# The three-bit rounding of the weights' lower words on VectorE, and the first tiles' steps listed anew, in an attention and SoLU feed-forward kernel

## The chip, the core and the metric

The kernel runs on one NeuronCore of a Trainium2 chip. A core has TensorE (PE in the profile: matmuls, with PEld for their weight loads), VectorE (DVE), ScalarE (ACT), GpSimd (POOL) and SyncE (SP, which here only issues DMAs). Each engine works through its own instructions in order; engines wait for one another by semaphores. The metric is the time of one execution in microseconds (us) on the device, as the median of several runs. Lower is better.

## The reference

Attention within chunks of 64 tokens, over 8 batches, 8 heads, 576 tokens and head size 64; its output, as 4608 rows of 512, goes through a feed-forward layer with a SoLU and a normalisation between two matrix products:

```python
scores = scale * np.matmul(q_c, k_c.transpose(0, 1, 2, 4, 3))
attn = softmax(scores)                      # over the 64 keys of the chunk
x = (attn @ v_c) as [4608, 512]
h = x @ w_in                                # 512 -> 1024
solu = h * softmax(h)
ln = (solu - mu) / np.sqrt(var + 1e-06) * g_ln
return (ln @ w_out).astype(np.float32)      # 1024 -> 512
```

The weights `w_in` and `w_out` come as 64-bit floats, q, k and v as 32-bit floats.

## The kernel before

**Tiles.** The 4608 rows are 36 tiles of 128 rows, numbered 0 to 35. Each tile goes through the same chain: q and k turned (head size on the partitions), 32 small score matmuls, softmax, the attention turned, 32 small value matmuls, `ffn_in` (L459: 24 matmuls of 128x512, since each operand is split into a high and a low part and three of the four products are taken), the SoLU (`solu_a` L479: a maximum over the row on VectorE, the exponential on ScalarE; `solu_b` L491: a product on VectorE, then a scale and shift called "Y ident" below), the result turned and split (`z_transpose` L562 or `z_turn` L527 with `z_split` L554), and `ffn_out` (24 matmuls, in three thirds of 8), scaled and stored.

**Weights.** The 64-bit weights are made into float pairs on the chip, in eight units of 1 MiB: units 0 to 3 are `w_in`, 4 to 7 `w_out`. A unit is loaded (`load_pair` L149, word P in the list below), its upper words are clamped and scaled (`unit_scale` L174, word c: min and max, then a ScalarE step called "prelu" below), its lower words are rounded to three bits (`unit_bits` L185, word b), both are joined on VectorE (`unit_join` L193, C), copied as the high part on ScalarE (`unit_high` L206, t), and the low part is the difference on VectorE (`unit_low` L219, d). The scaled unit lies in the tile `w_a`, of which there are two buffers, so a unit's c waits for the d of the unit two before it; the rounded words lie in `w_b`.

**Two parts of the program.** Tiles 5 to 35 have their `ffn_in` in a loop with a fixed order. All before it, which is the work on the weights, the attention of the first tiles, the `ffn_in` of tiles 0 to 4 and the `ffn_out` of tiles 0 and 1, is listed by hand in the string `START` (L18). Each word names a step and a tile or unit; a step of several parts stands once for each part, and every instruction is kept in that order on its engine. So `START` is an order for each of the five engines. The letters: n loads q and k of a tile in their natural layout, N turns one of them on TensorE and then evicts it (N:5:0 is q of tile 5), S scores, A softmax up to the exponential, B its sum and division, T turns the attention, V values with the split of x into high and low, M `ffn_in`, X `solu_a`, Y `solu_b`, R variance, z turns half of a result on TensorE, F one third of `ffn_out`, o store, Z, U and K turns by VectorE for the loop, v loads v, Q and q load q and k of a whole batch, w issues that many matmuls whose result nobody reads. F counts through: the first three are tile 0, the next three tile 1.

**Which engine.** `MOVED` (L34) names the words that do not run on their usual engine: c and b run on VectorE unless listed as `pool`, an eviction (N, z) on ScalarE unless listed as `dve`, Y ident on ScalarE unless listed. Before, b:0, b:1 and b:3 run on VectorE and the other five b on GpSimd; all eight c run on GpSimd.

**What ties the steps.** `ffn_in` writes the only buffer `ph` (L461), which is free again when Y of the tile before has read it on VectorE. The turned tiles of N, T and z share two PSUM banks (`bank`, L120) in rotation. The natural loads have two buffers, so n of a tile waits for the N of the tile two before it, and every load behind it on SP's queue waits too. `ffn_out` reads one pair `z_h`, `z_l`.

Of the kernel before, what the change touches and what calls it, by code (L numbers as in the profile page):

```python
# [15 lines left out]


START = """  # L18
n:0 P:0 P:0 n:1 P:1 w:5 N:0:0 N:0:0 w:1 N:0:1 N:0:1 w:3 S:0 n:2 c:0 A:0 A:0 w:7 N:1:0 b:0 v:0
c:1 c:0 B:0 w:2 N:1:1 N:1:0 N:1:1 C:0 P:2 w:3 S:1 t:0 c:2 T:0 T:0 c:1 A:1 A:1 w:4 N:2:0 w:2  # L20
N:2:1 n:3 N:2:0 b:1 w:2 V:0 P:3 N:2:1 S:2 d:0 C:1 t:1 V:0 b:2 v:1 B:1 n:4 w:2 T:1 T:1 d:1 A:2
c:2 A:2 V:0 C:2 w:9 N:3:1 N:3:1 N:3:0 N:3:0 M:0 M:0 B:2 b:3 t:2 S:3 n:5 c:3 c:3 d:2 C:3 V:1
N:4:0 N:4:0 t:3 T:2 N:4:1 N:4:1 n:6 A:3 A:3 d:3 M:0 B:3 N:5:1 T:2 M:0 N:5:0 P:4 V:1 S:4 N:6:0
N:5:1 N:5:0 X:0 X:0 v:2 g N:6:1 N:6:1 A:4 A:4 S:5 Y:0 c:4 c:4 T:3 T:3 V:1 A:5 A:5 N:6:0 b:4 n:7
C:4 P:5 Y:0 t:4 M:1 R:0 B:4 b:5 V:2 V:2 T:4 N:7:1 v:3 X:1 X:1 P:7 N:7:1 V:2 S:6 c:5 Y:1 c:5 T:4
d:4 v:6 v:7 B:5 V:3 Y:1 C:5 z:0:0 z:0:0 M:2 V:3 N:7:0 t:5 P:6 c:7 c:7 z:0:0 z:0:1 d:5 v:5 X:2
N:7:0 v:4 z:0:1 F X:2 V:3 z:0:1 c:6 c:6 Y:2 b:6 z:1:1 T:5 b:7 Q:2 q:8 T:5 C:7 Y:2 V:4 C:6 M:3
t:6 A:6 t:7 d:6 q:8 d:7 z:1:0 n:8 R:1 q:8 V:4 V:4 F F X:3 X:3 V:5 z:1:0 z:1:0 S:7 Y:3 Y:3 A:7
q:8 Z:2 A:7 Z:3 A:6 M:4 B:7 z:1:1 z:1:1 F F B:6 R:2 X:4 X:4 K:9 N:8:0 F Y:4 Y:4 U:6 U:7 V:5 o:0
o:1 V:5 N:8:0 R:4 N:8:1 N:8:1 R:3  # L30
"""


MOVED = """  # L34
N:6:0=dve N:8:1=dve Y:0=dve Y:4=pool b:2=pool b:4=pool b:5=pool b:6=pool b:7=pool c:0=pool
c:1=pool c:2=pool c:3=pool c:4=pool c:5=pool c:6=pool c:7=pool z:1:0=dve
"""


# [784 lines left out]
```

## Time and profile before

| | us |
|---|---|
| median of 3 runs | 488.02 (487.26 to 488.04) |
| the profiled execution | 488.82 |
| its span, first to last instruction | 487.0 |
| TensorE busy in the span | 468.7 |
| VectorE busy | 372.5 |
| ScalarE busy | 257.5 |
| GpSimd busy | 159.0 |

The span is the part of an execution that the profiler sees; 1.8 us lie around it. "Busy" is the time in which at least one instruction of the engine is under way. In the timeline a row is one instruction, or several like ones in a row, with its start and its length, and in brackets how long the engine sat idle before it and what released it. In the chain of waits each row is a piece of the chain that ended last, followed back from the end of the program.

### The profile page before, as it was taken

The page shows a single profiled execution, that of the slowest core. Times are in us where ns is not written, and L with a number is a line of the kernel's source. Part 1 is how long each engine was busy: PE and PEld are TensorE (multiplying, and loading weights), DVE is VectorE, ACT ScalarE, POOL GpSimd, SP SyncE. Part 2 cuts the span into 40 slices and gives each one's busy share as a digit, 9 for nine tenths or more (in the row PEclk, how much of TensorE's full clock was granted, in tenths as well). Part 3 has the DMA queues.
Part 4 walks back from the last instruction along what each step waited for, and adds up shares of the span by engine and source line. Part 5 has one row for each costly group of instructions (what it writes and reads, how often), then busy time and mean ns, then how long its engine had stood idle before and what let it go on. Part 6 is the DMA issues. An engine that isn't in the chain of part 4 may idle for free.

```text
span 487.0 us, 11097 instructions
## 1 busy us (share of the span) xinstructions
PE 468.7 (96%) x4208; PEld 384.7 (79%) x4208; DVE 372.5 (76%) x518; ACT 257.5 (53%) x424; POOL 159.0 (33%) x300
## 2 busy tenths in 40 slices
PE   8888887999999999999999999999999999999997
PEld 6666666888888888888888888888888888888876
DVE  3878759888869988888787879797979797954541
ACT  3867657564545564646464646464646464645452
POOL 1324570724231523232333323232323232323330
PEclk9989998999999999999999999999999999999999
DMA  9999994568776788687618596858762626153222
GB/s 261 276 201 263 238 153 62 157 106 193 141 191 125 191 153 194 121 181 151 186 35 209 96 203 129 206 97 178 154 173 48 170 56 164 47 150 84 74 60 86
DMA packets 194468, 72.57 MB, mean 149 GB/s; under 512 B 178224, under 2 KB 178992, under 8 KB 194032
## 3 DMA queue, kind: packets, MB, share of 16 engines
q1 hardware_dynamic: 187312, 58.23, 54.1%
q0 software_dynamic: 6528, 12.86, 10.4%
q8 instruction: 33, 0.54, 0.5%
q10 hardware_dynamic: 576, 0.79, 0.4%
q14 instruction: 19, 0.16, 0.1%
HBM read 36.70 MB, written 9.44 MB: 95 GB/s over the span
## 4 chain that ended last, share of the span: by engine, by line
PE 84%; POOL 4%; ACT 4%; DMA 3%; DVE 2%; issue 2%; SPq 1%; ACTq 0%; POOLq 0%; DVEq 0%
PE po L54 38%; PE ph L54 37%; PE tp L54 4%; PE sx L54 4%; POOL w_b L54 3%; DMA nat<-in_q_dram 2%; DMA w_raw<-in_moe_w_out_dram 1%; SPq L54 1%; ACT wo_h L54 1%; POOL w_a L54 1%; DVE w_a L54 1%; ACT z L54 0%; DVE h_nmax L54 0%; ACT sq L54 0%; ACT w_a L54 0%
## 5 line engine op out<-in xcount | busy, mean ns | idle before, releaser
L54 PE MATMUL po<-wo_l,z_h 128*128 128x512 f32 (+1 forms) x288 | 114.0, 396 | 2.4 <-DVE wo_l L54 2.4
L54 PE MATMUL ph<-wi_l,x_h 128*128 128x512 f32 x288 | 113.4, 394 | 1.5 <-DVE z L54 1.3
L54 ACT ACTIVATE z<-ph,h_nmax 128x1024 f32<-128x1024 f32 x36 | 40.2, 1116 | 137.6 <-DVE h_nmax L54 135.7
L54 PE MATMUL ph<-wi_h,x_h 128*128 128x512 f32 x288 | 112.6, 391 | 0.0
L54 PE MATMUL po<-wo_h,z_l 128*128 128x512 f32 (+1 forms) x288 | 112.3, 390 | 0.0
L54 PE MATMUL po<-wo_h,z_h 128*128 128x512 f32 (+1 forms) x288 | 112.1, 389 | 0.0
L54 POOL DMA_DIRECT2D z_t<-z_b x144 | 71.6, 505 | 32.1 <-DVE z_b L54 26.9
L54 POOL TENSOR_TENSOR u<-ssq,eps 128x1 f32<-128x1 f32 x36 | 6.8, 190 | 219.3 <-ACT sq L54 219.2
L54 PE MATMUL ph<-wi_h,x_l 128*128 128x512 f32 x288 | 78.3, 390 | 0.0
L54 DVE TENSOR_REDUCE h_nmax<-ph 128x1 f32<-128x1024 f32 x36 | 44.0, 1222 | 32.8 <-PE ph L54 32.8
L54 PEld LDWEIGHTS po<-wo_l,z_h 128*128 128x128 f32 x288 | 54.3, 189 | 14.8 <-DVE wo_l L54 2.8
L54 PEld LDWEIGHTS ph<-wi_l,x_h 128*128 128x128 f32 x288 | 54.3, 189 | 13.2 <-issue 1.4
L54 PEld LDWEIGHTS po<-wo_h,z_l 128*128 128x128 f32 x288 | 54.5, 189 | 11.8 <-DVE z_l L54 0.4
L54 PEld LDWEIGHTS ph<-wi_h,x_l 128*128 128x128 f32 x288 | 54.3, 189 | 11.4
L54 PEld LDWEIGHTS ph<-wi_h,x_h 128*128 128x128 f32 x288 | 54.4, 189 | 11.1
L54 PEld LDWEIGHTS po<-wo_h,z_h 128*128 128x128 f32 x288 | 54.4, 189 | 10.5
L54 DVE TENSOR_TENSOR z_l<-z_t,z_h 128x1024 fp32r<-128x1024 f32 (+1 forms) x37 | 42.1, 1137 | 25.4 <-ACT z_h L54 24.1
L54 DVE SCALAR_TENSOR_TENSOR z<-ph,z 128x1024 f32<-128x1024 f32 x36 | 43.9, 1221 | 13.6 <-ACT z L54 13.4
L54 ACT ACTIVATE z<-z,z_sum 128x1024 f32<-128x1024 f32 x34 | 39.2, 1153 | 23.5 <-DVE z L54 22.9
L54 DVE STREAM_TRANSPOSE z_b<-z 128x1024 f32<-128x1024 f32 x34 | 41.1, 1210 | 3.2 <-ACT z L54 3.1
L54 ACT CAST z_h<-z_t 128x1024 fp32r<-128x1024 f32 (+1 forms) x37 | 35.9, 971 | 6.5 <-PE po L54 6.5
L54 ACT ACTIVATE o_sb<-po,r 128x512 f32<-128x512 f32 (+1 forms) x36 | 24.3, 675 | 27.4 <-POOL r L54 18.6
(77 smaller groups left out, 609.5 us busy)
## 6 DMA issues: line engine op xcount, KB each, us to landing
out_dram<-o_sb SPq DMA_DIRECT2D x33, 256.0 KB, 2.5
v_sb<-in_v_dram SPq DMA_DIRECT2D x32, 256.0 KB, 4.5
z_t<-z_b SPq DMA_DIRECT2D x128, 64.0 KB, 2.9
z_t<-z_b POOLq DMA_DIRECT2D x128, 64.0 KB, 2.7
q_st<-in_q_dram SPq DMA_DIRECT2D x96, 72.0 KB, 3.0
k_st<-in_k_dram SPq DMA_DIRECT2D x96, 72.0 KB, 3.1
w_raw<-in_moe_w_out_dram SPq DMA_DIRECT2D x4, 1024.0 KB, 8.2
attn_t<-a_b SPq DMA_DIRECT2D x60, 64.0 KB, 4.0
```

The lines of the kernel that those rows point to most:

```text
L54: ins = make(*args, **kwargs)
```

## The change

Only the two strings differ. In `MOVED`, b:2, b:4, b:6 and b:7 are no longer listed, so that they run on VectorE; b:5 stays on GpSimd. Y ident of tile 0 goes from VectorE to GpSimd, that of tile 3 from ScalarE to VectorE and that of tile 4 from GpSimd to VectorE. The evictions N:6:0, N:8:1 and z:1:0 go from VectorE to ScalarE, N:0:1 and N:8:0 from ScalarE to VectorE.

`START` has the same steps in another order. It begins with unit 1 instead of unit 0, and its load stands ahead of the first loads of q and k. Unit 5 is loaded ahead of unit 4 and unit 6 ahead of unit 7; the number of idle matmuls (w) is 40 in both. The first lines and those around units 4 to 7:

```diff
 START = """
-n:0 P:0 P:0 n:1 P:1 w:5 N:0:0 N:0:0 w:1 N:0:1 N:0:1 w:3 S:0 n:2 c:0 A:0 A:0 w:7 N:1:0 b:0 v:0
+P:1 b:1 n:0 w:11 N:0:0 N:0:0 n:1 w:2 N:0:1 N:0:1 c:1 c:1 C:1 t:1 P:0 P:0 c:0 w:3 S:0 N:1:0
...
-N:5:1 N:5:0 X:0 X:0 v:2 g N:6:1 N:6:1 A:4 A:4 S:5 Y:0 c:4 c:4 T:3 T:3 V:1 A:5 A:5 N:6:0 b:4 n:7
-C:4 P:5 Y:0 t:4 M:1 R:0 B:4 b:5 V:2 V:2 T:4 N:7:1 v:3 X:1 X:1 P:7 N:7:1 V:2 S:6 c:5 Y:1 c:5 T:4
-d:4 v:6 v:7 B:5 V:3 Y:1 C:5 z:0:0 z:0:0 M:2 V:3 N:7:0 t:5 P:6 c:7 c:7 z:0:0 z:0:1 d:5 v:5 X:2
-N:7:0 v:4 z:0:1 F X:2 V:3 z:0:1 c:6 c:6 Y:2 b:6 z:1:1 T:5 b:7 Q:2 q:8 T:5 C:7 Y:2 V:4 C:6 M:3
-t:6 A:6 t:7 d:6 q:8 d:7 z:1:0 n:8 R:1 q:8 V:4 V:4 F F X:3 X:3 V:5 z:1:0 z:1:0 S:7 Y:3 Y:3 A:7
-q:8 Z:2 A:7 Z:3 A:6 M:4 B:7 z:1:1 z:1:1 F F B:6 R:2 X:4 X:4 K:9 N:8:0 F Y:4 Y:4 U:6 U:7 V:5 o:0
-o:1 V:5 N:8:0 R:4 N:8:1 N:8:1 R:3
+Y:0 S:4 N:6:0 N:6:0 N:5:1 V:2 A:4 V:2 V:2 T:3 T:3 M:1 A:4 g B:4 c:5 N:5:1 c:4 c:4 z:0:1 z:0:1
+b:4 N:6:1 N:6:1 n:7 v:3 v:4 S:5 X:1 X:1 T:4 T:4 N:7:1 N:7:1 b:5 z:0:1 A:5 A:5 V:3 P:6 c:6 Y:1
+Y:1 V:3 P:7 C:4 C:5 z:0:0 z:0:0 M:2 t:4 B:5 R:0 d:4 t:5 V:3 Q:2 q:8 z:0:0 c:7 N:7:0 N:7:0 S:6
+v:7 q:8 V:4 X:2 d:5 X:2 Y:2 T:5 T:5 V:4 b:6 b:7 c:6 v:5 C:6 c:7 C:7 t:6 q:8 z:1:1 n:8 F z:1:0
+t:7 R:1 d:6 d:7 M:3 X:3 X:3 F F v:6 Y:2 z:1:0 V:4 A:6 A:6 Y:3 Y:3 S:7 z:1:0 V:5 M:4 A:7 z:1:1
+o:0 R:2 B:6 A:7 z:1:1 Z:2 q:8 Z:3 F X:4 X:4 B:7 F F N:8:1 Y:4 V:5 V:5 U:6 U:7 N:8:1 R:3 Y:4
+N:8:0 R:4 N:8:0 K:9 o:1
 """
...
 MOVED = """
-N:6:0=dve N:8:1=dve Y:0=dve Y:4=pool b:2=pool b:4=pool b:5=pool b:6=pool b:7=pool c:0=pool
-c:1=pool c:2=pool c:3=pool c:4=pool c:5=pool c:6=pool c:7=pool z:1:0=dve
+N:0:1=dve N:8:0=dve Y:0=pool Y:3=dve Y:4=dve b:5=pool c:0=pool c:1=pool c:2=pool c:3=pool
+c:4=pool c:5=pool c:6=pool c:7=pool
 """
```

What the list gives each engine around this place, read off word by word:

- GpSimd before: c0 c1 c2 b2 c3 c4 b4, the variance R0, b5 c5 c7 c6 b6 b7, R1 R2. After: c1 c0 c2 c3 c5, Y ident of tile 0, c4 b5 c6 R0 c7 R1 R2.
- VectorE after, from X:1 to X:3: X1, low half of z0:1, A5, Y1, C4 C5 B5 d4, low part of x3, low half of z0:0, X2 d5 Y2 b6 b7 C6 C7 d6 d7 X3.
- TensorE after, from M:1: M1, z0:1, N6:1, S5, T4, N7:1, V3, z0:0, M2, N7:0, S6, V4, T5, z1:1, F, z1:0, M3, F F, S7, V5, M4, F F F, N8:1, N8:0, then the loop with tile 5. Before: M1, V2, T4, N7:1, S6, V3, z0:0, M2, N7:0, z0:1, F, z1:1, T5, V4, M3, z1:0, F F, V5, S7, M4, F F, N8:0, F, N8:1.
- SP before: n0 P0 n1 P1 n2 v0 P2 n3 P3 v1 n4 n5 n6 P4 v2 g n7 P5 v3 P7 v6 v7 P6 v5 v4, then batch 2 with n8. After: P1 n0 n1 P0 P2 v0 n2 n3 P3 n4 v1 n5 n6 v2 P5 P4 g n7 v3 v4 P6 P7, then batch 2 with v7, v5, n8 and v6 among it.

More of the change, by code (lines that the diff above doesn't have):

```diff
@@ L18 @@
 START = """
-n:0 P:0 P:0 n:1 P:1 w:5 N:0:0 N:0:0 w:1 N:0:1 N:0:1 w:3 S:0 n:2 c:0 A:0 A:0 w:7 N:1:0 b:0 v:0
[L20 to L23, printed above, removed]
-N:5:1 N:5:0 X:0 X:0 v:2 g N:6:1 N:6:1 A:4 A:4 S:5 Y:0 c:4 c:4 T:3 T:3 V:1 A:5 A:5 N:6:0 b:4 n:7
@@ new lines @@
+N:1:0 A:0 A:0 N:1:1 d:1 N:1:1 P:2 w:8 S:1 B:0 v:0 n:2 c:0 b:0 c:2 w:3 T:0 T:0 A:1 A:1 C:0 w:6
+V:0 c:2 t:0 B:1 w:6 N:2:1 V:0 N:2:1 b:2 V:0 N:2:0 N:2:0 n:3 w:1 N:3:0 N:3:0 S:2 C:2 d:0 P:3 T:1
+N:3:1 t:2 M:0 M:0 n:4 A:2 v:1 N:3:1 n:5 c:3 c:3 N:4:0 S:3 T:1 b:3 d:2 M:0 C:3 A:3 t:3 A:2 N:4:1
+N:4:1 d:3 N:4:0 V:1 V:1 N:5:0 n:6 v:2 N:5:0 A:3 M:0 B:2 T:2 V:1 P:5 T:2 X:0 X:0 B:3 P:4 c:5 Y:0
+Y:0 S:4 N:6:0 N:6:0 N:5:1 V:2 A:4 V:2 V:2 T:3 T:3 M:1 A:4 g B:4 c:5 N:5:1 c:4 c:4 z:0:1 z:0:1
+b:4 N:6:1 N:6:1 n:7 v:3 v:4 S:5 X:1 X:1 T:4 T:4 N:7:1 N:7:1 b:5 z:0:1 A:5 A:5 V:3 P:6 c:6 Y:1
```

## The prediction

> **What bounds the kernel now.** I read the page, then the chain of waits, then busy time by stage.
>
> ```profile
> span 487.0 us, 11097 instructions
> PE 84%; POOL 4%; ACT 4%; DMA 3%; DVE 2%; issue 2%; SPq 1%; ACTq 0%; POOLq 0%; DVEq 0%
> ```
>
> TensorE carries 84% of the chain. The rest has to be looked for where TensorE waits. I cut the span where the `ffn_in` of tiles 0, 1, 2, 3, 4, 5 begin (M0 to M5). Columns: stretch and length, then busy time (count) of PE, PEld, DVE, ACT, POOL, granted clock, DMA share, GB/s.
>
> ```profile
> 0.00:23.51 23.51, 20.07 (x209) 15.07 (x209) 13.71 (x20) 14.55 (x24) 5.82 (x14) 1.00 1.00 262
> 23.51:40.43 16.92, 13.91 (x187) 11.15 (x186) 13.27 (x19) 11.12 (x19) 4.92 (x3) 0.90 0.95 214
> 40.43:51.85 11.42, 9.20 (x134) 7.28 (x132) 8.91 (x15) 7.88 (x15) 7.24 (x5) 1.00 1.05 292
> 51.85:65.02 13.17, 10.55 (x80) 8.13 (x80) 10.21 (x14) 10.30 (x18) 7.62 (x5) 1.00 1.00 192
> 65.02:81.49 16.47, 12.82 (x109) 9.80 (x109) 10.75 (x15) 7.84 (x15) 5.74 (x4) 0.90 0.81 124
> 81.49:93.31 11.82, 11.82 (x56) 9.79 (x57) 11.53 (x18) 6.27 (x12) 5.70 (x11) 1.00 0.37 98
> 93.31:461.00 367.69, 367.67 (x3324) 304.60 (x3323) 296.48 (x411) 189.69 (x307) 116.83 (x253) 1.00 0.63 141
> ```
>
> From 93.31 TensorE is never idle for 367.7 us, and the change leaves that loop alone. So the change is worth what it shifts M5, less what the loop then has to wait for. In the first 93.31 us, TensorE idles in every stage but the sixth, most between M3 and M4. Chain and TensorE timeline say why:
>
> ```profile
> 40.96 3.72 POOL w_b L54
> 49.53 2.37 POOL w_b L54
> 62.58 3.71 POOL w_b L54
> 66.36 3.73 POOL w_b L54
> 74.51 0.49 PE L54 MATMUL po<-wo_l,z_h 128*128 128x512 f32 x1 [2.35 <-DVE wo_l L54]
> ```
>
> GpSimd's rounding is on the chain four times, 13.5 us in all. The last two keep the low parts of units 6 and 7 from `ffn_out`: TensorE idles 2.35 us at 74.51, and the stage's mean clock of 0.90 is that of 3.3 us at half clock (2 x 0.10 x 16.47), which cost half of that.
>
> **The change, part by part.** Prices first.
>
> ```profile
> L54 POOL TENSOR_SCALAR w_b<-w_raw x5: 3700/3717/3730, 21.9 to 66.4; 128x1024 uint32<-128x1024 uint32 x5
> L54 DVE TENSOR_SCALAR w_b<-w_raw x3: 682/682/687, 9.6 to 28.4; 128x1024 uint32<-128x1024 uint32 x3
> L54 POOL TENSOR_SCALAR z<-z,z_sum 128x1024 f32<-128x1024 f32 x1 | 1.1, 1138 | 2.3 <-DVE z L54 2.3
> L54 DVE TENSOR_SCALAR z<-z,z_sum 128x1024 f32<-128x1024 f32 x1 | 0.7, 748 | 0.0
> L54 DVE SCALAR_TENSOR_TENSOR w_a<-w_a,w_b 128x1024 uint32<-128x1024 uint32 x8 | 10.0, 1255 | 11.0 <-POOL w_b L54 9.9 <-ACT w_a L54 1.1
> L54 DVE SCALAR_TENSOR_TENSOR wo_l<-w_a,g_sb,wo_h 128x512 fp32r<-128x512 f32 x8 | 5.6, 746 | 0.4 <-ACT wo_h L54 0.4
> L54 ACT ACTIVATE wo_h<-w_a,g_sb 128x512 fp32r<-128x512 f32 x8 | 5.2, 716 | 7.2 <-DVE w_a L54 7.2
> L54 ACT ACTIVATE w_a<-w_a 128x1024 f32<-128x1024 f32 x8 | 8.4, 1056 | 4.3 <-POOL w_a L54 4.3
> L54 POOL TENSOR_SCALAR w_a<-w_raw 128x1024 f32<-128x1024 f32 x8 | 10.4, 1301 | 34.5 <-DMA w_raw<-in_moe_w_in_dram 17.2 <-DMA w_raw<-in_moe_w_out_dram 11.8 <-DVE wo_l L54 5.4
> L54 DVE TENSOR_REDUCE h_nmax<-ph 128x1 f32<-128x1024 f32 x36 | 44.0, 1222 | 32.8 <-PE ph L54 32.8
> L54 ACT ACTIVATE z<-ph,h_nmax 128x1024 f32<-128x1024 f32 x36 | 40.2, 1116 | 137.6 <-DVE h_nmax L54 135.7
> L54 DVE SCALAR_TENSOR_TENSOR z<-ph,z 128x1024 f32<-128x1024 f32 x36 | 43.9, 1221 | 13.6 <-ACT z L54 13.4
> L54 ACT CAST x_h<-sx 128x512 fp32r<-128x512 f32 x21 | 12.1, 576 | 0.1
> L54 ACT COPY attn_t<-tp 64x256 f32<-64x256 f32 x24 | 8.8, 365 | 0.7 <-PE tp L54 0.5
> L54 DVE TENSOR_REDUCE s_nmax<-sx 128x8 f32<-128x512 f32 x22 | 15.1, 688 | 7.2 <-PE sx L54 6.7
> 117.97 5.44 PE ph L54 x24
> 90.82 0.44 PE tp L54 x4
> 123.41 1.20 PE sx L54 x61
> ```
>
> Although seven of eight roundings will stand on VectorE, three stand there already: four move. GpSimd loses 4 x 3.72 = 14.9 us, VectorE gains 4 x 0.68 = 2.7. Y ident of tiles 3 and 4 costs VectorE 1.5 more, that of tile 0 gives it 0.75 back; the five moved evictions of about 0.7 leave it one less. VectorE thus pays 2.8 us net.
>
> I place the new lists on each engine with these durations, in order. 24 matmuls take 5.44 (a third 1.8), a turn 0.4, scores or values 0.6 each, an eviction on ScalarE 0.6, the four copies of a turned attention 1.5, a 512-wide step on VectorE 0.7, of which the next one overlaps 0.1.
>
> *Up to M1.* Loads are what the start waits on (DMA share 1.00, 262 GB/s: 4 us for 1 MiB). Unit 1 ahead of q and k puts the first turn some 3 us later, near 7.2; six more idle matmuls ahead of it fill about half of that. M0 needs unit 0 joined behind unit 1, two d on VectorE and the first values: about 23.4, as before. Its second half then sits behind N:4:0, which needs the bank that T1 holds; T1's copies (1.5 us) stand on ScalarE behind c3's prelu, so behind unit 3's load (near 25). N:4:0 comes near 28.9 after almost 3 us of idle TensorE, and I give it one stretch at half clock, as that stage has now (0.90: 3.4 us at half). M0 ends near 36.4. Maximum (1.2), T2's copies and exponential on ScalarE (to 39.6) and Y0 (1.2) free `ph`: M1 at 40.8, against 40.43. That is +0.4, give or take 1.6.
>
> *M1 to M2.* Y ident of tile 0 on GpSimd ends 42.0; z0:1 takes the turn at 46.3. The stage is now the loop through `ph`: matmuls to 46.3, maximum to 47.5, an eviction and exponential to 49.1, A5 on VectorE until 49.4, Y1 to 50.7, z0:0 turned (its bank free at 50.6): M2 at 51.0. That is 10.2 instead of 11.4. b4 on VectorE ends 45.1, where GpSimd would hold C4.
>
> *M2 to M3.* b5 stays on GpSimd behind c4: 43.3 to 47.0; C4 and C5 end 53.0, so it has 5 us of cover. Then d4 to 55.9, t5 on ScalarE behind t4 and R0 to 57.7, d5 to 59.6. F0 runs from 59.6, z1:0, M3 at 61.9: 10.9 instead of 13.2.
>
> *M3 to M4.* c6 waits for d5's buffer: 59.6 to 60.8; R0's two small steps, c7 to 63.0. b6 and b7 on VectorE end 62.0, preludes 62.6 and 64.1, C6 63.8, C7 65.3, t6 65.3, t7 66.7, d6 66.7, d7 68.1. F1 wants d6 at 67.4 and F2 wants d7 at 69.3: 0.7 and 1.2 us to spare. TensorE goes through M3 (67.4), F1 and F2 (71.2), S7 and V5: M4 at 72.5, 10.6 instead of 16.5, without the half clock. What is late next is VectorE: X3, A6 and Y3 follow d7 without a pause and free `ph` at 72.4.
>
> *M4 to M5.* Five and a half times two, two turns: 11.8, as now. M5 at 84.3.
>
> Some ten handovers on that path cost about 0.05 each (the first rounding above ends at 44.68, its join starts at 44.70; others show 0.1): M5 at 84.8, so 8.5 earlier.
>
> *Loads.* SP's queue issues unit 5 behind n6, which waits for N:4:1 (near 33.5), then unit 4.
>
> ```profile
> w_raw<-in_moe_w_out_dram SPq DMA_DIRECT2D x4, 1024.0 KB, 8.2
> 32.84 6.75 DMA w_raw<-in_moe_w_out_dram
> 40.94 0.58 SPq L54 DMA_DIRECT2D w_raw<-in_moe_w_out_dram  x1
> 67.85 9.42 SPq L54 DMA_DIRECT2D k_st<-in_k_dram  x16
> ```
>
> At 6.75 to 8.2 from issue they land near 41 and 44: c5 is then 41 to 42, c4 44 to 45, b5 ends near 49. Still inside the cover above. Units 6 and 7 land near 50 and 53, before c6 at 59.6. Batch 2's loads now have v7, v5, n8 and v6 among them, but start about 5 us sooner, so that the last are issued before 77.3 as now; K wants them near 87.
>
> *The loop's inputs.* U6 and U7 now stand behind x5's low part, so their end comes 1.2 us after M5 begins; before, 0.3 (93.57).
>
> ```profile
> 92.27 1.30 DVE L54 STREAM_TRANSPOSE a_b<-e 128x512 f32<-128x512 f32 x2
> attn_t<-a_b SPq DMA_DIRECT2D x60, 64.0 KB, 4.0
> 99.49 0.92 PE L54 MATMUL sx<-attn_t,v_sb 64*64 64x64 f32 x29
> ```
>
> Tile 6's values came 5.9 us after that end without idle; four issues of about 0.6 and 4.0 to landing say the data came just in time. The cost is between nothing and 1.0; I take 0.7, being nearer the full lag. Sum: 8.5 - 0.7 = 7.8. Span 479.2, its run 488.82 - 7.8 = 481.0; that run lies 0.8 above the median, so **488.02 - 7.8 = 480.2**.
>
> A row that speaks against the move:
>
> ```profile
> 25.82 2.09 POOL L54 TENSOR_SCALAR w_a<-w_raw 128x1024 f32<-128x1024 f32 x1 [0.17 <-DMA w_raw<-in_moe_w_in_dram]
> ```
>
> This c took 2.09 instead of 1.15, beside a join on VectorE. The Trainium skill ("SBUF — State Buffer", "Who interferes with whom") says that VectorE, in a two-port mode or with two SBUF inputs, locks GpSimd out for the whole instruction; by that, b6 and b7 hold c7 up to 0.7 more, inside the spare 1.2, and if that is gone the time is 480.9. The row agrees.
>
> **Rivals.** *VectorE takes over.* By my lists it works 44.7 of the 48 us from M0's end to M5 (five maxima 5.7, five products 6.2, four A 5.3, five B 7.9, b, C and d of the weights 11.7, eight low halves 4.9, two turns 2.3, Y ident 0.7). Before, from 40.43 to 93.31, it worked 41.4 of 52.9 (the four rows' sum), idle 11.5. If a third of that idle, 3.8, comes back as waits for ScalarE: 484.0. For: no other engine is so full. Against: its rows idle mostly for GpSimd's rounding (9.9 of 11.0 before joins).
>
> *The clock holds.* TensorE's 3 us pause near 27 may pass without half clock. The 3.4 us at half clock cost 1.7 there; without them 478.5. The Trainium skill ("TensorE: Matmul & The Clock Gate", "Part 1: The HAM clock gate") has the clock halve after an idle window of about 3.4 us; by that a pause of 3 us would pass, and the time would be 478.5. The trace is stricter: 2.35 us was enough.
>
> *Slower: SP's queue.* Unit 4 and 5 stand behind n6, n6 behind N:4:1, and Y ident of tile 0 now stands on GpSimd behind c5; TensorE's next step after M1 needs it. From unit 4 landing later than about 47, each us costs one; from 9 us later than that, near 56, the gain is gone, and at 58 the time is about 490. It takes N:4:1 near 46 instead of 33; nothing in the trace points there, and DMA share 0.95 leaves no room to catch up.
>
> *Nothing changes.* If units 6 and 7 landed too late for c6, the shorter b would be hidden. Unit 6's load took 10 us at most and c6 waited for a buffer (5.4, `wo_l`), so: 488.
>
> **How the numbers follow.** Forecast 480.2: 0.60; VectorE 484.0: 0.20; clock 478.5: 0.10; slower 490: 0.06; no change 488: 0.04. Best case: from M1 TensorE has 6 x 5.44 and about 8 us of small work, 40.7 against my 43.5; with M1 unmoved 477, and with some of the 1.7 as well 476. Worst inside the range: VectorE's case with 1.5 us lost before M1, 485.5. A measurement tells 0.2%, 1 us, from no change. Faster 0.90, same 0.04, slower 0.06.
>
> **What would show it.** M4 near 72.5 and M5 near 85, no idle of TensorE on `wo_l`, no half clock after M1, four roundings of 0.68 more on VectorE, no idle before joins on `w_b`. Wrong would be M1 later than 43, or c6 and c7 waiting for loads; a gap before tile 6's values over 1 us would mean that the loop pays back more than I charge.

## The result, and the profile after

The changed kernel takes **480.51 us** (median of 4 runs, 479.18 to 481.39) against 488.03 (487.26 to 489.48) for the kernel before, run beside it: a ratio of 0.9844, 95% interval 0.9804 to 0.9884. It is faster by 7.5 us, and the time lies 0.3 above the forecast. The profiled execution took 481.18 with a span of 479.4.

The head of the page and its chain of waits, to be set against 487.0 us, 4% POOL and 2% DVE:

```profile
span 479.4 us, 11110 instructions
PE 82%; DVE 7%; ACT 4%; DMA 3%; issue 1%; SPq 1%; POOL 0%; ACTq 0%; POOLq 0%
```

GpSimd has left the chain and VectorE has come onto it. The busy time by stage, cut again where the `ffn_in` of tiles 0 to 5 begin (M0 to M5), with the first third of tile 2's `ffn_out` as the end of the last stretch:

```profile
0.00:23.97 23.97, 20.06 (x208) 14.87 (x209) 15.67 (x22) 13.38 (x20) 4.68 (x13) 1.00 1.03 263
23.97:39.17 15.20, 12.66 (x183) 9.49 (x181) 13.09 (x18) 10.55 (x21) 1.51 (x1) 1.00 1.16 234
39.17:52.27 13.10, 10.40 (x109) 8.47 (x109) 10.89 (x15) 9.82 (x20) 7.44 (x4) 0.91 0.97 269
52.27:63.09 10.82, 10.82 (x114) 9.06 (x113) 10.16 (x16) 9.42 (x19) 2.97 (x4) 0.95 1.00 176
63.09:73.48 10.39, 10.39 (x107) 8.44 (x106) 9.79 (x14) 8.86 (x15) 0.74 (x2) 1.00 0.96 146
73.48:85.29 11.81, 11.81 (x62) 9.85 (x57) 11.64 (x18) 4.84 (x11) 4.91 (x10) 1.00 0.83 159
85.29:93.42 8.13, 7.98 (x156) 6.58 (x154) 6.97 (x10) 4.76 (x10) 3.43 (x8) 1.00 0.87 185
```

Read it beside the seven rows of before, stage by stage:

| stage | before | forecast | after |
|---|---|---|---|
| M0 begins | 23.51 | 23.4 | 23.97 |
| M0 to M1 | 16.92 | 17.4 | 15.20 |
| M1 to M2 | 11.42 | 10.2 | 13.10 |
| M2 to M3 | 13.17 | 10.9 | 10.82 |
| M3 to M4 | 16.47 | 10.6 | 10.39 |
| M4 to M5 | 11.82 | 11.8 | 11.81 |
| M5 begins | 93.31 | 84.8 (0.5 of it handovers) | 85.29 |

From M2 on, TensorE is busy for the whole of three stages (10.82 of 10.82, 10.39 of 10.39, 11.81 of 11.81). Two of them were full of waits before. Pieces of the chain say what stands on it now:

```profile
44.18 1.60 DVE s_e L54
45.79 1.54 DVE w_b L54
47.33 1.13 DVE h_nmax L54
...
66.43 2.65 DVE wo_l L54 x4
69.08 1.13 DVE h_nmax L54
...
88.02 3.71 DMA attn_t<-a_b
```

No rounding on GpSimd is left in it. The low parts of units 6 and 7 (66.43) are followed without a gap by tile 3's maximum (69.08). The last row is the loop's own transfer, of which more below. The VectorE timeline shows the two roundings that were 3.71 and 3.73 us on GpSimd, and the join behind them:

```profile
62.24 1.29 DVE L54 TENSOR_SCALAR w_b<-w_raw 128x1024 uint32<-128x1024 uint32 x2
64.07 1.23 DVE L54 SCALAR_TENSOR_TENSOR w_a<-w_a,w_b 128x1024 uint32<-128x1024 uint32 x1 [0.53 <-ACT w_a L54]
```

Both take 1.29 us together, and the join waits for ScalarE's prelude (0.53), no longer for a rounding.

### The profile page after: what moved, and what is told of

Its sections match the earlier page's. It is cut to its first block, busy times and chain, and to the rows that moved or that the text cites. A ratio compares the mean times of both kernels' runs of the same rounds, so it can differ in the third digit from the quotient of the medians.

```text
span 479.4 us, 11110 instructions
## 1 busy us (share of the span) xinstructions
PE 466.7 (97%) x4208; PEld 383.8 (80%) x4208; DVE 377.2 (79%) x522; ACT 256.4 (53%) x424; POOL 143.5 (30%) x296
## 4 chain that ended last, share of the span: by engine, by line
PE 82%; DVE 7%; ACT 4%; DMA 3%; issue 1%; SPq 1%; POOL 0%; ACTq 0%; POOLq 0%
PE po L54 38%; PE ph L54 36%; PE sx L54 4%; PE tp L54 4%; DMA w_raw<-in_moe_w_in_dram 1%; DVE h_nmax L54 1%; DMA nat<-in_q_dram 1%; ACT attn_t L54 1%; DVE e L54 1%; DVE z L54 1%; DMA attn_t<-a_b 1%; ACT z L54 1%; SPq L54 1%; DVE wo_l L54 1%; DVE w_a L54 1%
## 5 line engine op out<-in xcount | busy, mean ns | idle before, releaser
L54 DVE SCALAR_TENSOR_TENSOR z<-ph,z 128x1024 f32<-128x1024 f32 x36 | 43.9, 1221 | 13.1 <-ACT z L54 13.1
L54 ACT ACTIVATE z<-z,z_sum 128x1024 f32<-128x1024 f32 x33 | 38.0, 1152 | 22.2 <-DVE z L54 21.6
```

The lines of the kernel that those rows point to most:

```text
L54: ins = make(*args, **kwargs)
```

## The experiments

Two theories stood against each other. *Theory 1*: the gain is the roundings' move off GpSimd. *Theory 2*: it is the new order of the steps, and the moves add little. In what follows "the moves" are those of the four roundings; "the list" is all the rest, the order together with the moved Y ident steps and evictions. Beside them three smaller questions were open: why the stage M1 to M2 grew, whether the full VectorE costs anything, and what the half clock costs. "Changed" below is the kernel after the change; the ratio is to the kernel before, run on the same chip.

| kernel | median us (range, runs) | ratio, 95% interval |
|---|---|---|
| E1 new list, five b on GpSimd | 486.11 (485.53 to 487.10, 10) | 0.9963, 0.9945 to 0.9980 |
| E2 old list, one b on GpSimd | 485.05 (484.03 to 486.11, 10) | 0.9941, 0.9922 to 0.9961 |
| E10 changed, only b:6 and b:7 moved | 480.08 (479.21 to 480.43, 5) | 0.9832, 0.9808 to 0.9856 |
| E3 changed, b:4 later | 479.25 (478.80 to 480.72, 6) | 0.9826, 0.9800 to 0.9852 |
| E4 changed, b:5 on VectorE | 479.60 (478.43 to 480.47, 6) | 0.9827, 0.9800 to 0.9854 |
| E8 changed, b:4 on GpSimd, b:5 on VectorE | 480.02 (478.67 to 481.01, 4) | 0.9852, 0.9827 to 0.9878 |
| E5 changed, Y ident of tile 3 on ScalarE | 479.31 (479.00 to 480.09, 4) | 0.9837, 0.9822 to 0.9851 |
| E9 both of E8 and E5 | 479.42 (478.40 to 484.04, 6) | 0.9837, 0.9803 to 0.9871 |
| E6 changed, first q and k ahead of unit 1 | 480.37 (480.03 to 483.25, 4) | 0.9869, 0.9840 to 0.9898 |
| E7 changed, pauses filled | 480.05 (479.88 to 480.21, 4) | 0.9849, 0.9835 to 0.9864 |
| E11 changed, again | 480.51 (480.38 to 481.21, 5) | 0.9849, 0.9828 to 0.9870 |
| E12 changed, pauses filled, again | 480.46 (479.54 to 481.71, 5) | 0.9849, 0.9825 to 0.9874 |

### Which part makes the gain

**E1: the new list with the old places of the roundings.**

```diff
-N:0:1=dve N:8:0=dve Y:0=pool Y:3=dve Y:4=dve b:5=pool c:0=pool ...
+N:0:1=dve N:8:0=dve Y:0=pool Y:3=dve Y:4=dve b:2=pool b:4=pool b:5=pool b:6=pool b:7=pool c:0=pool ...
```

> The changed kernel with b:2, b:4, b:6 and b:7 put back on GpSimd; its list of steps stays. Theory 1, that the four roundings make the gain: GpSimd then has 4 x 3.72 us more in front of c6 and c7, tile 3's ffn_in to tile 4's grows from 10.4 towards the 16.5 of before, and the time is 485 to 487. Rival, that the new list makes it: the roundings b6 and b7 stand ahead of c6 and run while c6 waits for its buffer anyway, so c6 comes about 2 us later than now (near 60 instead of 56.8) and the time is 481 to 482.5.

Measured: 486.11, as Theory 1 had it, so the new list by itself is worth 1.5 us (487.58 for the kernel before beside it). The chain of E1 between M2 and M4:

```profile
60.21 1.12 POOL w_a L54
61.40 3.74 POOL w_b L54
65.22 4.74 POOL w_b L54
69.99 1.23 DVE w_a L54
```

The upper words of unit 7 are scaled, then units 6 and 7 are rounded one after the other, and only then comes unit 7's join. Before, GpSimd's last rounding ended at 70.09 (66.36 and 3.73 quoted in the prediction); here it ends at 69.96, the same place. The stage M3 to M4 is the old one too:

```profile
61.97:78.60 16.63, 13.27 (x107) 10.14 (x104) 9.77 (x13) 9.45 (x16) 8.66 (x4) 0.79 0.99 153
```

It takes 16.63 (16.47 before). Where the expectation speaks of b6 and b7 standing ahead of c6, that was misread: they stand behind c6, R0 and c7, as the chain shows.

**E2: the old list with the roundings moved.**

```diff
-N:6:0=dve N:8:1=dve Y:0=dve Y:4=pool b:2=pool b:4=pool b:5=pool b:6=pool b:7=pool c:0=pool
+N:6:0=dve N:8:1=dve Y:0=dve Y:4=pool b:5=pool c:0=pool
```

> The kernel before with b:2, b:4, b:6 and b:7 on VectorE and nothing else changed. Theory 1: the wait on wo_l (2.35 us) and the half clock behind it go, c6's 61.35 is followed by a join near 65 instead of 70.1, and the time is 482 to 484. Rival, that the list makes the gain: other waits hold the same places, 486.5 to 488.

Measured: 485.05, outside the 482 to 484 that Theory 1 gave. The moves by themselves are worth 2.5 us, and 1.5 + 2.5 = 4.0 is not 7.5 (by the ratios of the table, 1.8 + 2.9 against 7.6). Two places in E2 show what holds it. The chain between M2 and M3 (which begin at 51.01 and 64.18 here):

```profile
46.63 1.05 ACT sq L54 x2
...
48.67 3.03 POOL w_b L54
```

On GpSimd the old list has tile 0's variance R0 ahead of b5 and c5. R0 waits for ScalarE's square (46.63), so b5 starts at 48.67 and unit 5 is late whatever happens to the other roundings: M2 to M3 keeps its 13.17. The VectorE timeline between M3 and M4:

```profile
65.37 2.36 DVE L54 SCALAR_TENSOR_TENSOR w_a<-w_a,w_b 128x1024 uint32<-128x1024 uint32 x2
67.65 0.68 DVE L54 TENSOR_REDUCE s_nmax<-sx 128x8 f32<-128x512 f32 x1
68.36 0.69 DVE L54 TENSOR_TENSOR e<-sx,s_nmax 128x512 f32<-128x512 f32 x1
68.97 2.73 DVE L54 SCALAR_TENSOR_TENSOR wo_l<-w_a,g_sb,wo_h 128x512 fp32r<-128x512 f32 x4
...
72.81 1.22 DVE L54 TENSOR_REDUCE h_nmax<-ph 128x1 f32<-128x1024 f32 x1
```

The joins end at 67.73, but the old list puts a softmax step of tile 6 between them and the low parts, and more behind. Tile 3's maximum starts at 72.81, when the matmuls it reads had ended near 69.9 (64.18 and 5.74 of the chain). M3 to M4 is 12.57, not 10.39. So neither theory holds alone: the list without the moves leaves the wait of M3 to M4, and the moves without the list leave the wait of M2 to M3 and 2.2 us of M3 to M4. Which of the steps that the list shifts is worth how much was not tried one by one: the place of R0 and that of the softmax step are read from the traces.

**E10: of the four moves, only b:6 and b:7.**

```diff
-N:0:1=dve N:8:0=dve Y:0=pool Y:3=dve Y:4=dve b:5=pool c:0=pool ...
+N:0:1=dve N:8:0=dve Y:0=pool Y:3=dve Y:4=dve b:2=pool b:4=pool b:5=pool c:0=pool ...
```

> The new list with b:6 and b:7 alone on VectorE; b:2, b:4 and b:5 stay on GpSimd as before. If these two make the gain: tile 3's ffn_in to tile 4's is 10.4 to 10.6 instead of the 16.6 of the run with all on GpSimd, tile 2's begins near 49.7, C5 waits some 1.5 us for b5 as there, and the time is 479.3 to 480.3, no worse than the changed kernel. If b:2 and b:4 are needed too: 481.5 or more.

Measured: 480.08, within the changed kernel's spread, and 6.0 below E1 (6.4 by the ratios), which differs by b:6 and b:7 alone. E10's stages from M1 to M4:

```profile
39.11:49.95 10.84, 9.44 (x109) 7.75 (x109) 8.63 (x13) 9.14 (x18) 8.36 (x5) 1.00 0.99 239
49.95:62.37 12.42, 10.57 (x115) 8.58 (x114) 10.88 (x17) 9.81 (x20) 5.73 (x5) 1.00 0.98 217
62.37:72.86 10.49, 10.42 (x107) 8.47 (x106) 9.89 (x15) 8.95 (x15) 0.74 (x2) 1.00 0.94 154
```

M3 to M4 is 10.49 with two roundings moved. With b4 and b5 one after the other on GpSimd, M2 comes earlier (10.84) and M3 later (12.42); the two stages together take 23.26, against 23.92 in the changed kernel's profile and 22.70 in E12's. The moves of b:2 and b:4 give nothing that these runs can tell.

### Why the stage M1 to M2 grew

VectorE and GpSimd stand side by side there. In the changed kernel's VectorE timeline the division of tile 4's softmax (`s_e`) and the moved b4:

```profile
44.18 1.60 DVE L54 TENSOR_TENSOR s_e<-e,s_rinv 128x512 f32<-128x512 f32 x1
45.71 1.62 DVE L54 TENSOR_SCALAR w_b<-w_raw 128x1024 uint32<-128x1024 uint32 x1
```

and in its GpSimd timeline c4 and b5:

```profile
44.10 1.13 POOL L54 TENSOR_SCALAR w_a<-w_raw 128x1024 f32<-128x1024 f32 x1 [1.11 <-DMA w_raw<-in_moe_w_out_dram]
45.31 4.07 POOL L54 TENSOR_SCALAR w_b<-w_raw 128x1024 uint32<-128x1024 uint32 x1
```

`s_e` starts 0.08 after c4 and takes 1.60, b4 starts 0.40 after b5 and takes 1.62. The row in the prediction has 0.68 for a rounding on VectorE, and `s_e` takes 0.69 in E3 and E5. Three kernels take one neighbour or the other away.

**E3: b:4 later, just ahead of its join.**

```diff
-b:4 N:6:1 N:6:1 n:7 ...
-Y:1 V:3 P:7 C:4 C:5 ...
+N:6:1 N:6:1 n:7 ...
+Y:1 V:3 P:7 b:4 C:4 C:5 ...
```

> The changed kernel with the word b:4 moved from ahead of X:1 to just ahead of C:4, so that it no longer runs beside GpSimd's b5. If b4's 1.62 us (against 0.69 for the other roundings) comes from running beside b5: b4 takes 0.68 again, X1 starts about 1.5 us sooner, tile 2's ffn_in begins near 50.7 instead of 52.3, and the time is 479.0 (1.5 less than 480.5). If b4 is slow for another reason, such as loads landing: it stays at 1.6 in its new place and the time is within 0.5 of 480.5.

**E4: b:5 on VectorE too**, by dropping `b:5=pool`.

> The changed kernel with b:5 on VectorE too, in its place of the list, so that GpSimd rounds nothing. If the two engines get in each other's way: b4 takes 0.68 instead of 1.62 although it stands where it stood, the product of B4 still 1.6 (it runs beside c4), X1 comes 0.9 sooner, b5 costs VectorE 0.6, and the time is 480.0 to 480.5. If not: b4 stays at 1.6 and the time is 481.1.

The VectorE timeline of E4 at that place:

```profile
43.79 1.17 DVE L54 TENSOR_TENSOR s_e<-e,s_rinv 128x512 f32<-128x512 f32 x1
44.89 0.70 DVE L54 TENSOR_SCALAR w_b<-w_raw 128x1024 uint32<-128x1024 uint32 x1
```

With no b5 on GpSimd, b4 takes 0.70 in the same place. In E3 it takes 0.69 where it now stands, and tile 1's maximum starts at 45.08 instead of 47.25. So the neighbour on GpSimd is the cause of the long steps. Which step it strikes differs between executions of one kernel. E11 below is the changed kernel again, and in its profile b5 runs from 44.31 for 3.73 us:

```profile
44.40 1.58 DVE L54 TENSOR_TENSOR s_e<-e,s_rinv 128x512 f32<-128x512 f32 x1
45.91 0.68 DVE L54 TENSOR_SCALAR w_b<-w_raw 128x1024 uint32<-128x1024 uint32 x1
```

There `s_e` is long beside b5, and b4 has its usual length although b5 is still running; the last section works out when a step is struck. The times of E3 and E4 move little: 479.25 and 479.60, some 1 us below the changed kernel, in overlapping intervals. For E4 that is better than its 480.0 to 480.5. E3 came near its 479.0, but M2 came at 51.53 instead of 50.7: TensorE waited 1.56 us for a copy on ScalarE there, and its profile has the half clock.

**E8: b:4 on GpSimd and b:5 on VectorE.**

```diff
-... Y:4=dve b:5=pool c:0=pool ...
+... Y:4=dve b:4=pool c:0=pool ...
```

> The changed kernel with b:4 on GpSimd and b:5 on VectorE. The run with all roundings on GpSimd had tile 2's ffn_in at 49.7 instead of 52.3: there B4's product was followed by X1 at once. If b4 on VectorE costs the changed kernel that: X1 follows B4, tile 2's ffn_in begins near 50.0, tile 5's near 84.0, and the time is 478.7 to 479.3, as with both on VectorE or better. If the difference came from somewhere else in that run: tile 2's ffn_in stays past 51.5 and the time within 0.5 of 480.5.

Measured: 480.02. Tile 1's maximum follows `s_e` at once, at 45.16, and M2 begins at 50.09, M5 at 83.06, the earliest of all. E5's profile, which has b4 where the changed kernel has it and like E8's no half clock, has its maximum at 46.25, M2 at 50.59 and M5 at 83.56. A maximum that comes 1.1 us earlier is therefore worth 0.5 us at M2: the rest was covered by other waits. E8's median does not show even that; 480.02 misses the 478.7 to 479.3 expected.

### Whether the full VectorE costs anything

**E5: Y ident of tile 3 back on ScalarE**, by dropping `Y:3=dve`.

> The changed kernel with Y ident of tile 3 back on ScalarE. If VectorE is what holds tile 5's ffn_in (its timeline from 64 us on shows no idle time until 87.8): the 0.66 us that this step takes of it are won, tile 4 to tile 5 shortens only if TensorE was not full there (it was: 11.81 of 11.81), so at most the turns Z2, Z3 and what follows come 0.66 sooner and the time is 479.8 to 480.5. If TensorE holds it: no change, 480.5 give or take 0.5.

**E9: E8 and E5 together.**

```diff
-... Y:0=pool Y:3=dve Y:4=dve b:5=pool c:0=pool ...
+... Y:0=pool Y:4=dve b:4=pool c:0=pool ...
```

> The changed kernel with b:4 on GpSimd, b:5 on VectorE and Y ident of tile 3 on ScalarE. Alone, the first two brought tile 5's ffn_in to 83.1 in the profile and the third to 83.6 (85.3 in the changed kernel, with half clock in it). If they add: about 82.9, and 478.3 to 478.9. If they share the same slack: 479.0 to 479.5.

One window of the changed kernel, from unit 6's join to VectorE's first pause:

```profile
64.07:89.60 25.53, 25.53 (x176) 21.04 (x175) 25.29 (x36) 16.19 (x30) 8.54 (x19) 1.00 0.87 160
```

VectorE works 25.29 of 25.53 us, and TensorE all 25.53. Taking a 0.75 us step off VectorE in E5 leaves M3 to M4 at 10.48 and M4 to M5 at 11.81: nothing was waiting for it. E5's 479.31 lies below both answers of its expectation. All four of its executions had the full clock (0.999 or 1.000), which the changed kernel had in three of nine, and beside the 479.80 of those three it is 0.5 less, which such spreads do not separate. E9's 479.42 is the answer "the same slack": its M5, 84.08, is no earlier than E8's 83.06.

### The half clock

The changed kernel's windows of 1 us show TensorE at half clock, where the forecast had none after M1:

```profile
46.00:47.00 1.00, 0.43 (x32) 0.29 (x21) 1.00 (x1) 1.00 (x3) 1.00 (x1) 1.00 1.26 225
47.00:48.00 1.00, 0.65 (x4) 0.42 (x4) 1.00 (x2) 0.28 (x1) 1.00 (x1) 1.00 1.27 202
48.00:49.00 1.00, 0.00 (x0) 0.00 (x0) 1.00 (x3) 0.50 (x1) 1.00 (x1) 1.00 1.02 237
49.00:50.00 1.00, 0.66 (x4) 0.42 (x4) 0.97 (x3) 0.97 (x4) 0.38 (x1) 0.97 0.96 377
50.00:51.00 1.00, 0.56 (x20) 0.56 (x24) 1.00 (x2) 0.95 (x3) 0.00 (x0) 0.50 1.03 414
51.00:52.00 1.00, 1.00 (x27) 0.88 (x20) 1.00 (x4) 0.98 (x3) 0.00 (x0) 0.50 1.03 414
52.00:53.00 1.00, 1.00 (x5) 0.90 (x4) 1.00 (x2) 1.00 (x2) 0.00 (x0) 0.50 1.02 406
53.00:54.00 1.00, 1.00 (x5) 0.79 (x4) 1.00 (x2) 1.00 (x3) 0.00 (x0) 0.82 1.07 319
```

(1 - clock) summed over these rows and doubled is 2 x (0.03 + 3 x 0.50 + 0.18) = 3.4 us at half clock. It does not come in every execution: the granted clock over the whole run was 0.996 in two of the four runs (481.18, 481.39) and 1.000 in the other two (479.18, 479.84). 3.4 us at half clock lower the mean by 1.7 of 479, which is that 0.996.

**E7 and E12: unread matmuls in TensorE's pauses** (3, 5 and 3 of them, ahead of T4, N:7:1 and V3), with **E11**, the changed kernel itself, beside E12.

```diff
-... S:5 X:1 X:1 T:4 T:4 N:7:1 N:7:1 b:5 z:0:1 ...
+... S:5 y:3 X:1 X:1 T:4 T:4 y:5 N:7:1 N:7:1 y:3 b:5 z:0:1 ...
+    def fill(n):
+        m = ident_r.unsqueeze(1).to_broadcast([P, 4, P])
+        po = ps_o.tile([P, DM], F32, name="po")
+        for _ in range(n):
+            pe.matmul(
+                po.rearrange("p (x m) -> p x m", x=4), ident_r, m, start=True, stop=True
+            )
```

> The changed kernel with 3, 5 and 3 matmuls whose result nobody reads, put ahead of T4, N:7:1 and V3, where TensorE idles 0.9, 1.1 and 0.7 us between tile 1's and tile 2's ffn_in. If those pauses are what brings the half clock in some executions: every execution shows a clock of 1.00 (the four of the changed kernel have 0.996, 1.000, 0.996, 1.000) and none is over 480; the median is 479.3, about 1.2 less than 480.5, although TensorE does more. If the half clock comes by itself: clocks as mixed as before, 480.5 or a little more.

> The changed kernel once more, as the measure for the run with the filled pause beside it. If the half clock is a matter of chance in this kernel: a part of the executions at a clock of 0.996 and 481 to 481.5, the rest at 1.00 and 479 to 480.

> The changed kernel with the filled pause once more. If the pause brings the half clock: no execution under a clock of 0.999 and none over 480.5, beside the changed kernel that shows some. If not: as many low clocks as there.

Two windows of E12 at the same place:

```profile
48.00:49.00 1.00, 1.00 (x8) 0.78 (x7) 0.96 (x3) 1.00 (x3) 0.62 (x1) 1.00 0.97 340
51.00:52.00 1.00, 1.00 (x6) 0.83 (x5) 1.00 (x2) 1.00 (x2) 0.00 (x0) 1.00 1.03 418
```

The filling does what it should: the mean clock was 0.999 or 1.000 in all nine executions with it, against 0.996 in six of nine of the changed kernel. The time does not follow: 480.46 against 480.51 for E11 beside it, and 480.05 in E7, where 479.3 was expected. Of the changed kernel's nine executions the six at 0.996 average 480.89 and the three at 1.000 average 479.80, so the half clock costs about 1.1 us when it comes. That is an average of few: in E11 the one at full clock, 480.38, is next to three at 0.996 (480.41, 480.51, 480.64). E12's five, all at full clock, reach from 479.54 to 481.71. What spreads them is not shown by a profile of one of them and stays open.

### Unit 1 ahead of the first q and k

**E6: the load of tile 0's q and k back in front.**

```diff
-P:1 b:1 n:0 w:11 ...
+n:0 P:1 b:1 w:11 ...
```

> The changed kernel with the loads of tile 0's q and k issued ahead of unit 1's load. If unit 1 first is of use, the join C1 comes 2 us later than now (11.4 instead of 9.45) and tile 0's ffn_in, now at 23.97, comes near 25: 481.5. If the start is held by the sum of the loads and not by their order: 23.5 to 24.5 and the time within 0.5 of 480.5.

Measured: M0 begins at 26.65 instead of 23.97, later than either answer had it (near 25, or 23.5 to 24.5), and M1 at 40.12 instead of 39.17. The time, 480.37, lies inside the changed kernel's spread; beside the mean of its three full-clock executions, 479.80, it is 0.6 more. So of 2.7 us lost before M0, 1 us is left at M1, and the median can hardly tell it.

## Why the prediction was right

**The mechanism.** The forecast put the gain at the wait for units 5, 6 and 7, and there it is: M2 to M3 10.82 (forecast 10.9), M3 to M4 10.39 (10.6), M4 to M5 11.81 (11.8), full TensorE in all three, no rounding on GpSimd in the chain. E1 confirms it by putting the wait back.

**M0 to M1 was forecast too long: 17.4 against 15.2.** The step that failed is "Its second half then sits behind N:4:0, which needs the bank that T1 holds". The TensorE timeline of the changed kernel:

```profile
27.63 0.63 PE L54 MATMUL tp<-ident,nat 128*128 128x128 f32 x4 [0.66 <-DMA nat<-in_q_dram]
...
30.45 0.60 PE L54 MATMUL tp<-ident,nat 128*128 128x128 f32 x4
```

N:4:0 runs at 27.63 after 0.66 us of idle, waiting for its data and for no bank; forecast was 28.9 after almost 3 us. T1's copies ran behind it (from 28.81 on ScalarE), so it took the other bank, whose eviction had begun at 24.31 and taken 0.59. It is N:4:1 (30.45) that came right behind T1's copies. Without that pause there was no half clock in this stage either (1.00 in its row), where I had charged one.

**M1 to M2 was forecast too short: 10.2 against 13.1.** The step that failed is the loop through `ph` with its price of 0.7 a step. I had found that VectorE and GpSimd get in each other's way, and applied it to c7 alone. It struck two steps of VectorE on the chain, `s_e` and b4, by 0.9 each (1.60 and 1.62 against 0.69 in E3 and 0.70 in E4). Then came the half clock (0.91 in that row): the values and the turn ahead of M2 took 1.83 (50.44 to 52.27), against 1.15 in E5, which had the full clock (49.44 to 50.59). Together that is some 2.5 of the 2.9. The two errors, 2.2 too long and 2.9 too short, nearly cancelled by luck: M5 came 0.5 later than forecast. The total was closer than its parts.

**What each part is worth.** The prediction credited the moves and treated the list as what they run in. E1 and E2 price the list at 1.5 and the moves at 2.5 alone, and both together are 7.5. What it said of b4, that "GpSimd would hold C4", did not matter: E10 leaves b4 on GpSimd and loses nothing in the time. The two roundings of units 6 and 7 carry all of the moves' share that these runs can tell.

**The loop's inputs cost less than charged.** Tile 6's turned attention landed at 91.73 (88.02 and 3.71 in the chain) and its values ran at 91.86, two of their matmuls at 91.44. M5 came 8.02 earlier than before and the span is 7.6 shorter, so the loop pays back 0.4, where the forecast had 0.7.

**The rivals.** *VectorE takes over* did not happen from M2 on, though VectorE is as full as that rival said: TensorE has no wait there, and E5 shows that no one waits for the step it takes off. Between M1 and M2 TensorE does wait for VectorE, 1.12 and 0.67 us, behind the two long steps. *The clock holds* was half right. The pause it spoke of had shrunk to 0.66 us, and the half clock fell in another place, in some executions only. The three executions without it average 479.8, not 478.5. Two numbers about the clock bear on the page named there: the Trainium skill ("TensorE: Matmul & The Clock Gate", "Part 1: The HAM clock gate (the "warmup" mystery)") gives one idle window of about 3.4 us before the clock halves, on a window that runs free of the kernel. The 3.4 us at half clock and the change from execution to execution agree with such a window. A wholly idle one was not needed: from 46 to 50 TensorE was busy 1.74 of 4 us (0.43, 0.65, 0.00 and 0.66 in the rows of 1 us). The length of the pauses does not decide alone: E11's profile, with 0.27, 0.79 and 0.67 us at the three places, has the half clock (0.50 from 50 to 53), E5's, with 0.30, 0.88 and 0.67, has none. *SP's queue* held: c4 and c5 started at 44.10 and 40.64, near the forecast's 44 and 41.

## What to carry to other kernels

A step taken off a slow engine is worth what the wait it ends is worth in the order that the other engines then run: test the move and the new order apart, because here 1.5 and 2.5 alone made 7.5 together. Before a step goes to VectorE, look at what GpSimd begins in the microsecond before, since a price from an undisturbed row can more than double there. And when a total comes out right, compare the stages: two wrong steps can hide in it.

## What the runs showed of the hardware

**A rounding on GpSimd holds VectorE up in its first microsecond only.** E9 and E8 both have b5 on VectorE beside b4 on GpSimd. In the timelines of E9:

```profile
46.32 3.73 POOL L54 TENSOR_SCALAR w_b<-w_raw 128x1024 uint32<-128x1024 uint32 x1
46.49 1.50 DVE L54 TENSOR_SCALAR w_b<-w_raw 128x1024 uint32<-128x1024 uint32 x1
```

and in those of E8:

```profile
44.76 4.10 POOL L54 TENSOR_SCALAR w_b<-w_raw 128x1024 uint32<-128x1024 uint32 x1
46.29 0.68 DVE L54 TENSOR_SCALAR w_b<-w_raw 128x1024 uint32<-128x1024 uint32 x1
```

The same instruction beside the same neighbour takes 1.50 in one and 0.68 in the other. The Trainium skill ("SBUF — State Buffer", "Who interferes with whom") has the engine that comes first hold the shared ports for the whole instruction. `s_e` agrees: it began 0.08 after c4 and ended 0.55 after it (45.78 against 45.23), near its own 0.69. The roundings do not: b4 ended at 47.33, 2 us before b5 on GpSimd did (49.38).

The times fit a shorter hold. In E9 VectorE's rounding ended 1.67 after GpSimd's began (47.99 against 46.32); less its own 0.68, that is a hold of 0.99. E11's `s_e` also ended 1.67 after b5 began (45.98 against 44.31), and b4 behind it, 1.60 after that start, was not held. In E8 VectorE's rounding began 1.53 after GpSimd's, and it was not held either. Where `s_e` is still running when GpSimd's rounding starts, it is GpSimd that is held first: b5 takes 4.07 in the changed kernel, 0.34 more than 3.73, and 4.30, 0.57 more, in E5, and b4 ends 2.02 and 2.24 after its start, later by just as much. The profiles of E6, E7 and E12 give the same hold. Why GpSimd's rounding gives way after 1 us of its 3.7 was not tried and stays open.
